# A fused attention and soft mixture kernel: first pair of batches in halves, sums moved from POOL to PE, routing and merge rewritten

## The chip, the cores and the metric

The kernel runs on one core of a Trainium2 chip. The core has TensorE (PE, with its weight loads shown apart as PEld), VectorE (DVE), ScalarE (ACT), GpSimd (POOL) and SyncE (SP), which issues the transfers. The metric is the device time in microseconds from start to end of one execution; the time of a kernel is the median of its runs.

## The reference

```python
def _attn_ref(q, k, v, phi):            # 8 batches, 8 heads, 576 rows, 64 wide; phi has 32 columns
    a = phi - np.max(phi, axis=2, keepdims=True)      # softmax of phi over the 576 rows
    a = np.exp(a)
    a = a / (np.sum(a, axis=2, keepdims=True) + 1e-09)
    k_m = np.einsum('bhsm,bhsd->bhmd', a, k)          # 32 pooled keys and values for each head
    v_m = np.einsum('bhsm,bhsd->bhmd', a, v)
    scores = (1.0 / np.sqrt(q.shape[-1])) * np.matmul(q, k_m.transpose(0, 1, 3, 2))
    ...                                               # softmax over the 32
    return np.matmul(attn, v_m)

def _moe_ref(x, phi, w1, w2):           # x: 4608 x 512; phi: 512 x 32 slots; 8 experts of 4 slots
    logits = x @ phi
    d = exp(logits - logits.max(0)); d /= d.sum(0) + 1e-09     # over the 4608 rows
    slot_input = d.T @ x
    ...                                               # each expert: relu(slot_input[e] @ w1[e]) @ w2[e]
    c = exp(logits - logits.max(1)); c /= c.sum(1) + 1e-09     # over the 32 slots
    return c @ slot_out                               # 4608 x 512
```

The attention output x is never formed. The slot logits come from the attention weights times (v_m times slot phi), and the slot input from the attention weights times the routing weights.

## The kernel before

Work is handed to a small planner, class Plan: every `add(engine, cost, fn, r, w, also, pri, dma)` is one group of instructions with a cost in us, the tiles it reads and writes, and a due time set by `plan.at`. At the end `plan.issue()` goes through the groups by its own costs and so fixes the order of the instructions on each engine and of the transfers in the one DMA queue of SP. Buffers are rings of Slots; a group waits for a slot until its last user is done. The order is set when the program is made. What the chip does later follows that order with semaphores.

The eight batches go in four pairs (bp 0 to 3; g is 0 or 1 in a pair). A batch's rows lie on 128 partitions in four column blocks c (two heads, a = 0 and 1, each), nine rows j per partition. For each batch:

- `pool_phi`: load phi; DVE takes the maximum over j (L511), a PE transpose (L519), a small DVE maximum (L524) and PE matmuls (L533) spread it; ScalarE copies it (L544); POOL subtracts it (L549); ScalarE takes the exponential in place (L555); POOL adds the nine j by a tree of four additions (L562); a PE matmul with a mask of the half partitions (L572) and two DVE operations (L579, L580) give the reciprocal sums.
- `pool_kv`: load k and v; 144 PE matmuls of 64 x 32 weights (L599) accumulate the pooled keys and values in kvbank, of which there is one; ScalarE scales them out (L615, L622); PE transposes (L635, L640); ScalarE copies (L654, L645); PE multiplies the pooled values with the slot phi (L662); ScalarE places the result (L675).
- `load_q`, `q_blocks`: load q, two DVE transposes (L700), one for each half of the columns.

For each c of a pair: `scores` (PE L716, DVE transpose out of PSUM L730), `softmax` (DVE maximum L746, POOL subtract L751, ScalarE exponential L756, DVE sum L761, ScalarE L766, DVE reciprocal L770, POOL multiply L774, DVE transpose L777) and `logits` (PE L785), which accumulates the slot logits of the pair in one PSUM bank. DVE turns those into L (L955). `route` then takes the maximum over the rows for each slot: a strided DVE reduction of L (L803), PE transpose (L810), DVE (L815), PE (L821), DVE subtracts (L829), ScalarE exponential (L837); then 36 matmuls with the attention weights (L849), copies (L861, L865), matmuls (L875, L881), a masked DVE product (L890) and the matmuls that give the pair's unnormalised slot input sip (L909).

After the last pair the four pairs' parts are merged with factors from their maxima (DVE L969 to L1000; L975 is ScalarE's exponential): SIU and SD hold the parts of slot input and denominator, SIM is the merged slot input. The experts follow: `expert_in` (L1064), `hidden`, `expert_out` (L1113) read 32 weight tiles of 1 MB each; `slots` makes the combine weights; the tail multiplies them with the experts' output (L1220) and writes 12 pieces.

Memory: one arena of 44288 columns holds the attention tiles (`stack`) from the bottom up, and the weight tiles (`ws`, 2048 columns each, 19 of them) over the same columns from the top down. A weight load waits until every attention tile under its slot is done.

The first loads have an order of their own:

```python
FIRST = ["phi0", "phi1", "mphi", "q0", "k0", "v0", "q1", "k1", "v1"]
```

`fill` puts matmuls on ones into PE's idle time early (to 25 us of the planner's clock) and before the experts (L476).

Of the kernel before, what the change touches and what calls it, by code (L numbers as in the profile page):

```python
# [252 lines left out]
def kernel(  # L253
# [103 lines left out]
    def stack(shape, n, fifo=False):  # L357
# [37 lines left out]
    kvs = stack([KV_SZ], 2, fifo=True)  # L395
# [14 lines left out]
    C_EXP = 0.8  # L410
# [22 lines left out]
    add(DVE, 1.8, f, r=[ident_b], w=[maskhp_b, maskc_b, rep_b, ones_b])  # L433
# [6 lines left out]
    dmhs = sb("dmh", [NS, 1], 2)  # L440
# [22 lines left out]
    FIRST = ["phi0", "phi1", "mphi", "q0", "k0", "v0", "q1", "k1", "v1"]  # L463
# [37 lines left out]
    def pool_phi(b):  # L501
        pt = phis.tile()
        ph = lambda: pt.ap.rearrange("p (c j m) -> p c j m", c=C, j=J)
        load(
            lambda: pt.ap.rearrange("p (c x) -> p c x", c=C), rows(phi, b), H * S * M * 4, pt,
            pri=first(f"phi{b}"),
        )
        mx, mh, mb, es, rs = pmxs.tile(), pmhs.tile(), pmbs.tile(), pess.tile(), prss.tile()
        add(
            DVE, 2.2,  # L510
            lambda: nc.vector.tensor_reduce(  # L511
                mx.ap, ph().rearrange("p c j m -> p c m j"), axis=AX.X, op=ALU.max
            ),
            r=[pt], w=[mx],
        )
        t0 = b_m.tile()
        add(
            PE, TP,
            lambda: nc.tensor.transpose(t0.ap[:, :P], mx.ap.rearrange("p c m -> p (c m)"), ident),  # L519
            r=[mx, ident_b], w=[t0], also=[mh],  # L520
        )
        add(
            DVE, dve(P),
            lambda: nc.vector.tensor_reduce(  # L524
                mh.ap, t0.ap[:, :P].rearrange("x (a p) -> x a p", a=2), axis=AX.X, op=ALU.max
            ),
            r=[t0], w=[mh],
        )
        t1 = b_m.tile()

        def f():
            for a in range(2):
                nc.tensor.matmul(  # L533
                    t1.ap[HALF * a: HALF * a + HALF, :P],
                    mh.ap[:, a: a + 1].to_broadcast([P, HALF]),
                    ident,
                    start=True,
                    stop=True,
                )

        add(PE, pe(4, HALF, P, tiles=2), f, r=[mh, ident_b], w=[t1], also=[mb])
        add(
            ACT, act(128),
            lambda: nc.scalar.copy(mb.ap.rearrange("p c m -> p (c m)"), t1.ap[:, :P]),  # L544
            r=[t1], w=[mb],
        )
        add(
            POOL, pool_tt(PHI_SZ),
            lambda: nc.gpsimd.tensor_tensor(  # L549
                ph(), ph(), mb.ap.unsqueeze(2).to_broadcast([P, C, J, M]), op=ALU.subtract  # L550
            ),
            r=[mb, pt], w=[pt],
        )
        add(
            ACT, act(PHI_SZ, False), lambda: nc.scalar.activation(pt.ap, pt.ap, AF.Exp),  # L555
            r=[pt], w=[pt],
        )
        tr = trees.tile()

        def f():  # L560
            t = tr.ap
            plus = lambda o, x, y: nc.gpsimd.tensor_tensor(o, x, y, op=ALU.add)  # L562
            plus(t, ph()[:, :, 0:4, :], ph()[:, :, 4:8, :])
            plus(t[:, :, 0:2], t[:, :, 0:2], t[:, :, 2:4])
            plus(t[:, :, 0], t[:, :, 0], t[:, :, 1])
            plus(es.ap, t[:, :, 0], ph()[:, :, 8, :])

        add(POOL, pool_tt(512) + pool_tt(256) + 2 * pool_tt(128), f, r=[pt], w=[es, tr])
        sp = b_m.tile()
        add(  # L570
            PE, pe(2, 128, 2),
            lambda: nc.tensor.matmul(  # L572
                sp.ap[:, :2], es.ap.rearrange("p c m -> p (c m)"), maskhp, start=True, stop=True
            ),
            r=[es, maskhp_b], w=[sp], also=[rs], slack=S_SLACK,
        )

        def f():
            nc.vector.tensor_scalar(rs.ap, sp.ap[:, :2], EPS, None, op0=ALU.add)  # L579
            nc.vector.reciprocal(rs.ap, rs.ap)  # L580

        add(DVE, 0.32, f, r=[sp], w=[rs])
        return pt, ph, rs

    def pool_kv(b, pt, ph, rs, vpb):

        kb = kvs.tile().split(2)
        kv = lambda: kb.ap.rearrange("p (i c x) -> p i c x", i=2, c=C)
# [91 lines left out]
        for r in range(R):  # L680
            add(ACT, act(H * NS), lambda f=f, r=r: f(r), r=[vpp], w=[vpb.part(R * g + r)])
# [594 lines left out]
```

## Time and profile before

| what | value |
|---|---|
| time, median of 3 runs | 222.75 us (222.53 to 223.4) |
| profiled execution | 221.83 us, of which 220.1 us are the span |
| busy: PE, PEld | 172.5, 105.3 us |
| busy: DVE | 135.5 us |
| busy: ACT | 71.4 us |
| busy: POOL | 86.7 us |
| read from HBM, written | 66.65 MB, 9.44 MB |

Busy time is the time in which an engine has an instruction at work, and a wait inside the order of its queue counts as idle. The span runs from the first to the last instruction. In a row of the timeline stand the start, the time it took in us, engine, line, operation, tiles and shapes, and how long the engine was idle before it and for what. In the table of groups stand the busy us of the whole group, the mean ns of one, and the idle time before them.

### The profile page before, as it was taken

Reading aid. Unit: us, or ns where it says so; the run is one execution under the profiler, and the core shown is the slowest. Engines: PE = TensorE matmul, PEld = TensorE weight load, DVE = VectorE, ACT = ScalarE, POOL = GpSimd, SP = SyncE. Lnnn points to the kernel's source line nnn. Section 1 sums busy time; section 2 is a strip of 40 time slices with the busy share of each in tenths; the row PEclk is TensorE's granted clock in tenths of the full one; section 3 lists DMA queues with packets and bytes.
Section 4 is the critical chain, followed back from the end, with each engine's and each line's share of the span. In section 5 each row is a group of like instructions: output and inputs, shape, how many; then the busy total and the mean of one; then the engine's idle time right before and its main releaser. Section 6 shows DMA issues by size and latency. Waiting matters only on the chain.

```text
span 220.1 us, 5624 instructions
## 1 busy us (share of the span) xinstructions
PE 172.5 (78%) x2418; PEld 105.3 (48%) x2418; DVE 135.5 (62%) x230; ACT 71.4 (32%) x182; POOL 86.7 (39%) x85
## 2 busy tenths in 40 slices
PE   8997977695798988598988799629999975599400
PEld 6676745354564654356654387415554340065100
DVE  6825048969459999879658965499102860268500
ACT  2041234542516626337342340201002331168400
POOL 6298019596934992999623641030000000000000
PEclk9999999979699999999969999976999999769755
DMA  6999999999999999999596493999999998049997
GB/s 215 383 395 390 380 392 381 390 380 390 385 388 389 388 406 380 389 392 406 194 410 212 188 420 102 401 350 327 395 413 410 408 409 320 3 179 411 415 415 295
DMA packets 27881, 76.45 MB, mean 347 GB/s; under 512 B 1744, under 2 KB 5840, under 8 KB 27856
## 3 DMA queue, kind: packets, MB, share of 16 engines
q1 hardware_dynamic: 27856, 76.09, 91.1%
q8 instruction: 19, 0.31, 0.6%
q14 instruction: 6, 0.05, 0.1%
HBM read 66.65 MB, written 9.44 MB: 346 GB/s over the span
## 4 chain that ended last, share of the span: by engine, by line
PE 41%; DMA 22%; DVE 14%; POOL 9%; issue 5%; ACT 2%; SPq 1%; DVEq 0%; POOLq 0%
DMA top<-in_q_dram 10%; DMA arena<-in_moe_w_dram 9%; PE bank L1064 7%; PE kvbank L476 6%; PE bank L785 5%; PE scbank L716 4%; PE bank L1220 4%; PE kvbank L599 3%; DMA out_dram<-arena 3%; DVE arena L700 3%; POOL arena L774 3%; POOL arena L562 3%; PE bank L849 2%; PE kvbank L1113 2%; POOL arena L751 2%
## 5 line engine op out<-in xcount | busy, mean ns | idle before, releaser
L549 POOL TENSOR_TENSOR arena<-arena 128x1152 f32<-128x1152 f32 x8 | 21.0, 2632 | 16.0 <-ACT arena L544 13.3
L476 PE MATMUL kvbank<-ones 128*128 128x256 f32 x92 | 25.4, 419 | 2.2 <-ACT arena L622 1.1
L700 DVE STREAM_TRANSPOSE arena<-top 128x1152 f32<-128x1152 f32 x16 | 21.7, 1361 | 7.1 <-DMA top<-in_q_dram 7.1
L774 POOL TENSOR_TENSOR arena<-arena,ssm 128x576 f32<-128x576 f32 x16 | 18.5, 1162 | 15.6 <-DVE ssm L770 15.5
L562 POOL TENSOR_TENSOR arena<-arena 128x128 f32<-128x128 f32 (+2 forms) x32 | 23.4, 731 | 2.3 <-ACT arena L555 0.3
L716 PE MATMUL scbank<-arena 64*64 64x288 f32 x256 | 21.6, 433 | 3.0 <-DVE arena L730 2.5
L785 PE MATMUL bank<-arena 128*128 128x288 f32 x64 | 21.4, 464 | 2.6 <-DVE arena L777 2.6
L751 POOL TENSOR_TENSOR arena<-arena,smx 128x576 f32<-128x576 f32 x16 | 18.4, 1158 | 11.5 <-DVE smx L746 11.5
L599 PE MATMUL kvbank<-arena 64*32 64x128 f32 x1152 | 20.2, 273 | 2.2 <-issue 1.5
L476 PEld LDWEIGHTS kvbank<-ones 128*128 128x128 f32 x92 | 18.1, 207 | 6.7 <-issue 1.6
L511 DVE TENSOR_REDUCE arena<-arena 128x128 f32<-128x1152 f32 x8 | 17.0, 2138 | 5.6 <-DMA arena<-in_phi_dram 5.6
L599 PEld LDWEIGHTS kvbank<-arena 64*32 64x32 f32 x1152 | 16.2, 106 | 6.3 <-issue 3.9
L1064 PE MATMUL bank<-arena,SIM 128*32 128x256 f32 x256 | 16.4, 421 | 3.4 <-DVE SIM L1000 3.4
L1113 PE MATMUL kvbank<-arena 128*32 128x512 f32 x128 | 15.6, 598 | 2.9 <-DMA arena<-in_moe_w_dram 2.9
L730 DVE STREAM_TRANSPOSE arena<-scbank 128x576 f32<-128x576 f32 x16 | 12.2, 765 | 8.9 <-PE scbank L716 8.9
L785 PEld LDWEIGHTS bank<-arena 128*128 128x128 f32 x64 | 12.1, 206 | 8.1 <-DVE arena L777 3.8
L1220 PE MATMUL bank<-sr,cT 128*128 128x512 f32 x36 | 13.2, 505 | 3.1 <-DVE sr L1207 1.4
L1231 DVE COPY arena<-bank 128x512 f32<-128x512 f32 x18 | 11.8, 691 | 4.7 <-DMA out_dram<-arena 2.4
L777 DVE STREAM_TRANSPOSE arena<-arena 128x576 f32<-128x576 f32 x16 | 12.1, 758 | 3.8 <-POOL arena L774 3.7
L716 PEld LDWEIGHTS scbank<-arena 64*64 64x64 f32 x256 | 9.0, 137 | 10.8 <-DVE arena L730 4.5
L756 ACT ACTIVATE arena<-arena 128x576 f32<-128x576 f32 x16 | 11.0, 688 | 8.4 <-POOL arena L751 8.4
L1064 PEld LDWEIGHTS bank<-arena,SIM 128*32 128x32 f32 x256 | 8.6, 121 | 10.7 <-DVE SIM L1000 3.6
(104 smaller groups left out, 234.4 us busy)
## 6 DMA issues: line engine op xcount, KB each, us to landing
arena<-in_moe_w_dram SPq DMA_DIRECT2D x32, 1024.0 KB, 9.9
top<-in_q_dram SPq DMA_DIRECT2D x8, 1152.0 KB, 13.8
arena<-in_k_dram SPq DMA_DIRECT2D x8, 1152.0 KB, 11.2
arena<-in_v_dram SPq DMA_DIRECT2D x8, 1152.0 KB, 13.6
out_dram<-arena SPq DMA_DIRECT2D x12, 768.0 KB, 7.6
arena<-in_phi_dram SPq DMA_DIRECT2D x8, 576.0 KB, 8.7
arena<-in_moe_phi_dram SPq DMA_DIRECT2D x1, 64.0 KB, 4.8
```

The source lines that it names most:

```text
L476: lambda: nc.tensor.matmul(warm.ap, ones, ones.unsqueeze(1).to_broadcast([P, 2, P]), start=True, stop=True,),
L549: lambda: nc.gpsimd.tensor_tensor(ph(), ph(), mb.ap.unsqueeze(2).to_broadcast([P, C, J, M]), op=ALU.subtract),
L562: plus = lambda o, x, y: nc.gpsimd.tensor_tensor(o, x, y, op=ALU.add)
L599: nc.tensor.matmul(acc.ap[M * c: M * c + M, a, : 2 * D], ph()[h0: h0 + HALF, c, j, :], kv()[h0: h0 + HALF, :, c, j * D: j * D + D], start= ...
L700: nc.vector.transpose(qT.ap.rearrange("p (i u y) -> p u i y", i=2, y=Y), qt.ap[:, h * QT_SZ: h * QT_SZ + QT_SZ].rearrange("p (u i x) -> p ...
L716: nc.tensor.matmul(scb.ap[HALF * g: HALF * g + HALF, a, :JY], kb[g].ap[h0: h0 + HALF, i, c].rearrange("p r m -> p (r m)"), qT[g][c // 2].a ...
L751: lambda: nc.gpsimd.tensor_tensor(exv(), exv(), bc(mx), op=ALU.subtract),
L774: lambda: nc.gpsimd.tensor_tensor(exv(), exv(), bc(sm), op=ALU.mult),
L785: nc.tensor.matmul(lp.ap[:, :JY], vpb.ap[:, h, :], aT.ap[:, a * JY: (a + 1) * JY], start=(h == 0), stop=(h == H - 1),)
L1064: nc.tensor.matmul(hb.ap[NS * j: NS * j + NS, :256], SIM.ap[:, 2 * i + c, NS * e: NS * e + NS], wv[:, c, 256 * j: 256 * j + 256], start=(e ...
L1113: nc.tensor.matmul(pacc.ap[NS * x: NS * x + NS, 0, :DM], hT()[:, 4 * t + 2 * i + j, NS * e: NS * e + NS], wv[:, j, t, :], start=(e == 0 an ...
L1220: lambda po=po, i=i, ct=cT[bp, j0]: nc.tensor.matmul(po.ap[:, :DM], ct.ap()[:, i * P: i * P + P], sr.ap, start=True, stop=True),
```

## The change

1. The first pair is worked in two units: column blocks 0 and 1, then 2 and 3. Loads, maxima, subtraction, exponential, sums, pooling and transposes are issued for each unit; the other pairs keep one unit. The functions become methods of a class Batch (`load_phi`, `load_kv`, `load_q`, `turn_q`, `shifted`, `summed`, `pooled`, `turned`). The scores of c wait for the keys of their unit only, and the logits for the values of theirs. In the first loads q stands behind k and v of the unit.
2. The exponentials go to a tile of their own (pes), ordered by j first. The sums over the rows are made by PE: nine matmuls, with a 32-column mask as weights and the exponentials moving, then a ScalarE copy and one small matmul. POOL's tree goes.
3. kvs has three buffers for two; pes is new; the tree's buffer goes.
4. The routing maximum is taken from the logits in PSUM with the slots on partitions; its negative is spread by a matmul with rep, ScalarE's exponential reads PSUM with it as a bias, and DVE transposes the result. MB holds negatives of maxima.
5. In the merge the sums over the first three pairs are made ahead of the last pair's; the last pair's part is added to them with two DVE operations. The copy of one half of the last pair's wt goes from ScalarE to DVE. The zeroing of hTb goes from POOL to DVE.
6. Logits get a due time half a pair later.

```diff
-    dm1s = stack([NS], 2)
+    dTs = stack([JN], 1)
...
-    trees = stack([C, 4, M], 1)
-    pmxs, pmbs, pess = stack([C, M], 2), stack([C, M], 2), stack([C, M], 2)
+    pes = stack([J, C, M], 2)
+    pess = stack([C * M], 1)
+    pmxs, pmbs = stack([C, M], 2), stack([C, M], 2)
...
-    kvs = stack([KV_SZ], 2, fifo=True)
+    kvs = stack([KV_SZ], 3, fifo=True)
...
+        nc.vector.memset(maskw, 0.0)
...
-    FIRST = ["phi0", "phi1", "mphi", "q0", "k0", "v0", "q1", "k1", "v1"]
+    FIRST = [
+        "phi0.0", "phi1.0", "k0.0", "v0.0", "k1.0", "v1.0", "mphi", "q0.0", "q1.0",
+        "phi0.1", "phi1.1", "k0.1", "v0.1", "k1.1", "v1.1", "q0.1", "q1.1",
+    ]
...
+            add(
+                ACT, act(PHI_SZ // self.units, False),
+                lambda: nc.scalar.activation(
+                    pe_.ap[:, :, c0:c1].rearrange("p j c m -> p c j m"), ph(), AF.Exp
+                ),
+                r=[pt.part(u)], w=[pe_.part(u)],
+            )
+        def summed(self, u):
+            pe_, rs, n, o = self.pe, self.rs, self.n, u * self.n
+            s4, sp, es = b_m.tile(), b_m.tile(), pess.tile()
+            def f():
+                for j in range(J):
+                    x = Y * (j % 4)
+                    nc.tensor.matmul(
+                        s4.ap[x: x + Y, :n], maskw,
+                        pe_.ap[:, j, c0:c1].rearrange("p c m -> p (c m)"),
+                        start=(j < 4), stop=(j >= J - 4), tile_position=(0, x),
+                    )
+            add(PE, 0.45, f, r=[pe_.part(u), maskw_b], w=[s4], also=[es])
+            add(ACT, act(n), lambda: nc.scalar.copy(es.ap[:, :n], s4.ap[:, :n]), r=[s4], w=[es])
+            add(PE, 0.2, lambda: nc.tensor.matmul(
+                    sp.ap[o: o + n, :2], es.ap[:, :n], rep[:, 0, :2], start=True, stop=True),
+                r=[es, rep_b], w=[sp], also=[rs])
...
+        r=[*(x.qT[c // 2] for x in pair), *(x.kd.part(x.part(c)) for x in pair)],
...
+        add(PE, 0.96, f, r=[aT, *(vpb.part(4 * u + x) for x in range(4))], w=[lp])
...
+    def route(bp, ex, pair, lp):
+        def f():
+            nc.vector.tensor_reduce(dmx.ap[:, 0:1], lp.ap[:, :JY], axis=AX.X, op=ALU.max)
+            nc.vector.tensor_scalar(dmx.ap[:, 1:5], neg_b.ap, dmx.ap[:, 0:1], None, op0=ALU.mult)
...
+            PE, 0.12, lambda: nc.tensor.matmul(
+                t0.ap[:, :C], rep.rearrange("p a n -> p (a n)"), dmx.ap[:, 1:5], ...
+            DVE, 0.15,
+            lambda: nc.vector.tensor_reduce(dmx.ap[:, 5:6], t0.ap[:, :C], axis=AX.X, op=ALU.min),
+            ACT, act(JN),
+            lambda: nc.scalar.activation(dT.ap, lp.ap[:, :JY], AF.Exp, bias=dmx.ap[:, 5:6]),
+        add(DVE, dve(JN), lambda: nc.vector.transpose(df.ap, dT.ap), r=[dT], w=[df])
...
+            if bp == NSEG - 1 and g == 1:
+                add(DVE, dve(HM) + dve(1), lambda g=g: f_dve(g), r=[wp[g]], w=[wt.part(g)])
...
+        units = 2 if bp == 0 else 1
+        pair = [Batch(2 * bp + g, units) for g in range(2)]
+        for u in range(units):
+            for x in pair:
+                plan.at(bp - 1.15 + 0.5 * x.g + 0.25 * u, 8)
+                x.load_phi(u); x.shifted(u); x.load_kv(u); x.summed(u); x.pooled(u); x.turned(u, vpb)
+            plan.at(bp - 0.45 + 0.3 * u)
+            for x in pair:
+                x.load_q(u)
...
+            plan.at(bp + 0.25 * c + 0.5, 15)
+            logits(c, aT, vpb, pair[0].part(c), lp)
...
+        nc.vector.tensor_mul(rst.ap[:, 0], wtp.ap[:, 4 * NS: 5 * NS], cf.ap[:, nl])
+        nc.vector.tensor_add(rst.ap[:, 0], rst.ap[:, 0], st.ap)
+        nc.vector.reciprocal(rst.ap[:, 0], rst.ap[:, 0])
+        nc.vector.tensor_mul(rst.ap[:, 1], rst.ap[:, 0], cf.ap[:, nl])
+        nc.vector.tensor_mul(sip_c.ap, sip_c.ap, bc(rst.ap[:, 0]))
...
+        nc.vector.tensor_mul(SIT.ap, part, bc(rst.ap[:, 1]))
+        nc.vector.tensor_add(
+            SIM.ap.rearrange("p c (e x) -> p c e x", e=E)[:, :, :, :SE],
+            SIT.ap.rearrange("p c (e s) -> p c e s", e=E),
+            sip_c.ap.rearrange("p c (e s) -> p c e s", e=E),
...
-    add(POOL, 2.0, lambda: nc.gpsimd.memset(hTb.ap, 0.0), r=[SIM], w=[hTb])
+    add(DVE, 2.4, lambda: nc.vector.memset(hTb.ap, 0.0), r=[SIM], w=[hTb])
```

More of the change, by code (lines that the diff above doesn't have):

```diff
@@ L403 @@
     mphd_b = keep("mphd", [P, C, 2, NS])
-    ident, maskhp, maskc, rep, ones, mphd = (
-        x.ap for x in (ident_b, maskhp_b, maskc_b, rep_b, ones_b, mphd_b)
+    ident, maskw, maskc, rep, ones, mphd = (
+        x.ap for x in (ident_b, maskw_b, maskc_b, rep_b, ones_b, mphd_b)
     )
@@ L409 @@
     WC = 0.45
-    C_EXP = 0.8
     S_SLACK = 0.6
@@ L422, in f @@
         nc.vector.tensor_reduce(
-            maskhp, ident.rearrange("p (c x) -> p c x", c=2), axis=AX.X, op=ALU.add
+            maskw[:, :2], ident.rearrange("p (c x) -> p c x", c=2), axis=AX.X, op=ALU.add
         )
@@ L439 @@
     prss = sb("prs", [P, 2], 3)
-    dmhs = sb("dmh", [NS, 1], 2)
+    dmxs = sb("dmx", [P, 6], 2)
+    neg_b = keep("neg", [P, C])
+    add(
+        DVE, 0.1,
+        lambda: nc.vector.tensor_scalar(neg_b.ap, maskc, -1.0, None, op0=ALU.mult),
+        r=[maskc_b], w=[neg_b],
+    )
     L = [keep(f"L{i}", [P, JN]) for i in range(NBP)]
@@ L498, in rows @@
         return x[b].rearrange("h (p j) y -> (h p) (j y)", j=J).rearrange("(c r) x -> r c x", r=P)
[L501 to L538, printed above, removed]
-                )
[L541 to L583, printed above, removed]
@@ L709, in scores @@
+    def scores(c, pair, ex):
         scb = b_s2.tile()
@@ L879, in f @@
                     )
-            for g in range(2):
-                nc.tensor.matmul(
-                    wtp.ap[:, 4 * NS: 5 * NS],
-                    wt.ap[:, g, HM: HM + 1].to_broadcast([P, P]), rep[:, 0, :],
-                    start=(g == 0), stop=(g == 1),
-                )
         add(PE, 1.3, f, r=[wt, rep_b], w=[wtp], also=[wtb])
@@ L898, in route @@
         )
-        add(
-            ACT, act(32),
-            lambda: nc.scalar.copy(SD.ap[:, bp, :], wtp.ap[:, 4 * NS: 5 * NS]),
-            r=[wtp], w=[SD.part(bp)],
-        )
+        if bp < NSEG - 1:
+            add(
+                ACT, act(32),
+                lambda: nc.scalar.copy(SD.ap[:, bp, :], wtp.ap[:, 4 * NS: 5 * NS]),
+                r=[wtp], w=[SD.part(bp)],
+            )
         sip = b_m.tile()
@@ L915, in f @@
                     )
-        add(PE, 0.6, f, r=[wtb, *vm], w=[sip])
+        add(PE, 0.6, f, r=[wtb, *(x.vm for x in pair)], w=[sip])
         if bp == NSEG - 1:
-            return sip
+            return wt, wtp, sip
         add(
@@ L950 @@
             plan.at(bp + 0.25 * c, 15)
-            scores(c, qT, kb, ex)
+            scores(c, pair, ex)
             aT = softmax(c, ex)
-            logits(c, aT, vpb, lp)
-        add(
-            DVE, dve(JN), lambda lp=lp, bp=bp: nc.vector.transpose(L[bp].ap, lp.ap[:, :JY]),
-            r=[lp], w=[L[bp]],
-        )
+            plan.at(bp + 0.25 * c + 0.5, 15)
+            logits(c, aT, vpb, pair[0].part(c), lp)
         plan.at(bp + (1.2 if bp < NBP - 1 else 1.0), 10)
-        sip = route(bp, ex, vm)
+        last = route(bp, ex, pair, lp)
     plan.at(20)
@@ L965 @@
     st = keep("st", [P, NS])
+    rst = keep("rst", [P, 2, NS])
     nl = NSEG - 1
+    wt, wtp, sip = last
     def f():
-        nc.vector.tensor_reduce(m4.ap, MB.ap.rearrange("p b n -> p n b"), axis=AX.X, op=ALU.max)
+        nc.vector.tensor_reduce(m4.ap, MB.ap.rearrange("p b n -> p n b"), axis=AX.X, op=ALU.min)
         nc.vector.tensor_tensor(
```

447 lines of the change are left out of this document (276 added, 171 removed).

## Prediction

> **What bounds the kernel now.** I read the page's head first, then the chain of waits, then a table of stages that I cut at four instants, and last the timeline at the cuts. The head:
>
> ```profile
> span 220.1 us, 5624 instructions
> ...
> DMA  6999999999999999999596493999999998049997
> GB/s 215 383 395 390 380 392 381 390 380 390 385 388 389 388 406 380 389 392 406 194 410 212 188 420 102 401 350 327 395 413 410 408 409 320 3 179 411 415 415 295
> ...
> arena<-in_moe_w_dram SPq DMA_DIRECT2D x32, 1024.0 KB, 9.9
> top<-in_q_dram SPq DMA_DIRECT2D x8, 1152.0 KB, 13.8
> ...
> arena<-in_phi_dram SPq DMA_DIRECT2D x8, 576.0 KB, 8.7
> ```
>
> The transfers run at 380 to 415 GB/s nearly everywhere. They fail in two places: slices 20 to 25 (104.5 to 137.6 us), and slices 34 to 36, between the last weight and the first output. The cuts:
>
> ```profile
> 26.23 1.53 PEld L599 LDWEIGHTS kvbank<-arena 64*32 64x32 f32 x110 [0.48 <-DMA arena<-in_v_dram]
> 31.31 1.46 PE L716 MATMUL scbank<-arena 64*64 64x288 f32 x16
> 64.41 1.20 PE L716 MATMUL scbank<-arena 64*64 64x288 f32 x16
> 135.83 0.48 DVE L955 STREAM_TRANSPOSE L<-bank 128x288 f32<-128x288 f32 x1 [1.90 <-PE bank L785]
> 147.32 0.29 DVE L1000 TENSOR_TENSOR SIM<-arena,st 128x128 f32<-128x128 f32 x1
> 187.44 1.11 PE kvbank L1113 x8
> ```
>
> 31.3 is the first scores matmul of pair 0 (the two first batches), 64.4 that of pair 1, 135.8 the end of the last logits (I call it E), 147.6 the merged slot input SIM, 187.4 the last expert matmuls. Busy time between the cuts (engine, busy us, instructions; then clock, DMA share, GB/s):
>
> ```profile
> core 0: us, PE busy (x) PEld busy (x) DVE busy (x) ACT busy (x) POOL busy (x), PEclk, DMA share, GB/s
> 4.30:31.30 27.00, 23.98 (x387) 18.31 (x385) 12.83 (x14) 6.88 (x17) 11.63 (x13) 1.00 1.06 386
> 31.30:64.40 33.10, 25.37 (x564) 16.95 (x562) 23.67 (x35) 14.05 (x34) 25.59 (x23) 0.90 1.06 386
> 64.40:114.60 50.20, 43.06 (x770) 27.27 (x769) 43.53 (x69) 22.55 (x67) 34.58 (x31) 0.97 0.98 372
> 114.60:135.80 21.20, 19.43 (x170) 12.71 (x170) 15.00 (x26) 6.52 (x20) 9.16 (x8) 1.00 0.66 255
> ```
>
> VectorE (DVE) holds the attention stage: from 4.3 to 135.8 it works 95.0 us (the first four rows) of 131.5, only 12.8 of the first 27.0, and 87% of 64.4 to 114.6. After E the DMA rules, but it is late because weight slots come free only as attention lets go of its memory:
>
> ```profile
> 56.07 3.22 SPq L458 DMA_DIRECT2D arena<-in_moe_w_dram  x1
> ...
> 126.20 0.37 SPq L458 DMA_DIRECT2D arena<-in_moe_w_dram  x1
> 135.83 0.88 SPq L458 DMA_DIRECT2D arena<-in_moe_w_dram  x2
> ```
>
> Between the first two of these rows 14 of the 32 weight loads are issued; the 15th and 16th go out at E itself. The 18 that are left by then are 18.9 MB, 46 us at 410 GB/s (2.56 each), and 187.4 - 135.8 is 51.6. So the end follows E, until the DMA has no idle time left to give.
>
> **The change, part by part.**
>
> **Halves of the first pair.** Before, v of batch 1, the last of 8.26 MB (two batches, each of 576 KB of phi and 1152 KB each of q, k and v), is waited for until 26.2, and scores start 5.1 us behind. Afterwards scores of c = 0, 1 need only the first halves, 4.13 MB: 26.2 - 4.13/0.386 = 15.5, plus 3 us of q transposes and waits (an estimate between 0 and the 5.1 us from v): 18.5, 12.8 us earlier. The second halves land at 26.2 as before. The halves add the instructions of 2 more units (a second transpose, reduction, reciprocal each, the big ones at half size), which I put at 2 us of DVE; where units go through the single kvbank one behind another, ScalarE's copies stand between them, but that is work in a stretch in which DVE waits anyway. The first pair's DMAs become 16 for 8, in a queue whose issue is hidden behind the landing; q moves behind k and v, and the slot weights (mphi) behind them too, so POOL's copies of mphi (mphd) come later, beside POOL's first subtractions, and only the vpp matmuls wait for them.
>
> How much of 12.8 reaches E? DVE has 95.0 + 2 = 97 us to do. Up to 18.5 it does 6.7, at the first row's rate (12.83 in 27.0). The other 90.3 take 114 us at the share of 31.3 to 135.8 (82.2 of 104.5, 0.79), which gives E at 133; 104 at the 0.87 of the third row, E at 122. Which of them depends on the next part.
>
> **Phi sums by PE.** POOL's tree goes, PE and ScalarE take it up:
>
> ```profile
> DMA top<-in_q_dram 10%; DMA arena<-in_moe_w_dram 9%; PE bank L1064 7%; PE kvbank L476 6%; PE bank L785 5%; PE scbank L716 4%; PE bank L1220 4%; PE kvbank L599 3%; DMA out_dram<-arena 3%; DVE arena L700 3%; POOL arena L774 3%; POOL arena L562 3%; PE bank L849 2%; PE kvbank L1113 2%; POOL arena L751 2%
> L562 POOL TENSOR_TENSOR arena<-arena 128x128 f32<-128x128 f32 (+2 forms) x32 | 23.4, 731 | 2.3 <-ACT arena L555 0.3
> L572 PE MATMUL bank<-maskhp,arena 128*128 128x2 f32 x16 | 2.6, 235 | 0.0
> L849 PE MATMUL bank<-arena 64*32 64x288 f32 x144 | 7.5, 408 | 1.2 <-DVE m L969 1.2
> L519 PE MATMUL bank<-ident,arena 128*128 128x128 f32 x8 | 2.6, 321 | 6.2 <-DVE arena L511 5.9 <-DVE prs L579 0.3
> ```
>
> 23.4 us leave POOL, which alternates with DVE in every softmax (subtract, multiply); 3% of the span, 6.6 us, are on the chain of waits itself. In its place stand 9 matmuls of 128 x 32 weights with 128 columns, a copy and a 2-column matmul per batch. Low end: as L849, 7.5/144 = 0.05 us each, 0.5; high end: as L519 one behind another, 9 x 0.32 = 2.9. I take 0.6, since column-tiled L849 is the nearer form. With 0.24 for the small matmul and less the 0.33 of L572 it is 0.5 a batch net, 4 us on PE, 22 at the high end; PE has 16.6 us idle from 31.3 to 135.8. The change adds a wait there, the small matmul's for ScalarE's copy, with the kv matmuls and next scores queued behind it on PE, and DVE waiting for those; before, the same matmul waited for the tree's last addition. So I take DVE's share in between, at 0.83: 90.3/0.83 = 108.8, E at 18.5 + 108.8 = 127.3. E comes some 9 us earlier, at 127; bounds 3 and 14 us.
>
> [...]
>
> ```profile
> 105.89 1.17 PE bank L785 x4
> 107.06 0.87 PE kvbank L599 x48
> ```
>
> These two neighbours in the chain of waits differ in tiling (128*128, then 64*32), and no time shows between them. [...]
>
> **Exponentials past the mask, third kv buffer.** ScalarE's exp writes another tile (pes) in another order at the same size: nothing. That and a third kv buffer cost memory. By the diff's sizes the attention tiles grow from 34436 to 40932 of 44288 columns; with slots of 2048 columns, 4 weight slots are free from the start now and 1 afterwards. Once the last kv is used 10 are free now and 9 then, after the last scores 13 and 13. The DMA idles (410 - 255)/410 of the fourth row, 8 us, so I take 0 for the loss, and 3 x 2.56 = 7.7 us if nothing else makes it up.
>
> **Routing and merge,** E to SIM, 11.8 us now:
>
> ```profile
> 139.17 1.65 PE L849 MATMUL bank<-arena 64*32 64x288 f32 x36 [1.16 <-DVE m L969]
> 142.86 0.69 DVE L890 TENSOR_TENSOR arena<-bank,maskc 128x512 f32<-128x512 f32 x1 [1.84 <-PE bank L881]
> 144.38 2.02 POOL L1046 MEMSET arena<- 128x2304 f32 x1 [11.25 <-PE bank L909]
> 144.53 1.90 DVE L990 TENSOR_SCALAR st<-st 128x32 f32<-128x32 f32 x1
> 149.47 0.17 DVE L1148 TENSOR_SCALAR csm<-csm 128x9 f32<-128x9 f32 x1
> L579 DVE TENSOR_SCALAR prs<-bank 128x2 f32<-128x2 f32 x8 | 1.1, 141 | 2.0 <-PE bank L572 2.0
> 147.63 0.04 issue
> L837 ACT ACTIVATE arena<-arena 128x288 f32<-128x288 f32 x4 | 1.8, 455 | 0.7 <-DVE arena L829 0.7
> ```
>
> To the start of L849: 3.34 now. Then: reduction 0.48 (as L955, which reads the same PSUM columns), negative 0.14 (L579), matmul 0.24 (L572), small minimum 0.14, exp 0.46 (L837), transpose 0.48, six hand-overs at 0.04 (the issue row): 2.18. Gain 1.2. Further from their forms, these could be 0.5 more or less together. L849, copies (half of them moved to DVE) and L890 keep their time. From L890's end (143.55) to SIM's (147.6) it is 4.1 now: L990 sits 1.90 beside POOL's memset and ends with it, where its like, L1148, takes 0.17. Then: five small operations on DVE, some 1.2 (between 0.14 and 0.29 each), beside the sip matmuls, and two like L1000, 0.29 each, with hand-overs 1.9. Gain 2.2; E to SIM 8.4. The memset goes to DVE, behind SIM: 2 us, taken as on POOL, in front of DVE's routing work, behind which only the experts' hidden layer could wait, after the 16 us of its input matmuls. The slots freed at SIM come 3.4 us nearer to E; of the 5.5 us by which 51.6 exceeds the 46 of pure transfer I take 1.7 as saved (0 to 3.4).
>
> **Sum.** Last experts at 127 + 51.6 - 1.7 = 176.9 instead of 187.4; the tail of 32.7 us is untouched. Span 209.6, 10.5 less. The profiled execution took 221.83, the median of the runs is 222.75, 0.92 above: 222.75 - 10.5 = 212.2.
>
> **The rivals.**
> (1) The start is eaten. On the chain stands
>
> ```profile
> 22.68 14.10 DMA top<-in_q_dram
> ```
>
> q of batch 2, landing at 36.8, and its place behind 12.4 MB is not moved by halving. If pair 1 stays where it is, E comes only 3 us earlier: 218.0 with the merge. Against it: pair 1's scores start only at 64.4, long behind that landing, after pair 0's logits have had DVE and POOL.
> (2) The DMA floor. 33.1 MB at 386 GB/s from 4.3 to 90, then 32 loads at 2.56 us: 172, 173.4 with the landing; 206.1 of span, 208.7. It needs E at 123 or before, which is DVE at 0.87.
> (3) Slower: prefetch starves. If E stays and the three lost slots are missing at E, 11 loads are in instead of 14, and the last lands 7.7 later: 222.75 + 7.7 - 1.7 = 228.7. It decides once E moves by less than 6 us with all three missing. Against it: 10 against 9 slots, and the 8 idle us. PE at its high end (22 us against 16.6 idle) would help it along.
> (4) Nothing moves but the merge, and that is drowned: 221 to 223.
>
> **How the numbers follow.** Forecast 212.2 (E 5 to 12 us earlier, 209.5 to 216.5): 0.54. Rival 1 (216.5 to 221): 0.17. Rival 2 (208 to 209.5): 0.12. Rival 3: 0.11. Rival 4: 0.06. The range 208.0 to 219.5 leaves out rivals 3 and 4 and the upper edge of rival 1. A change of 0.5%, 1.1 us, is about what three runs from 222.53 to 223.4 can tell. Faster 0.83, same 0.06, slower 0.11.
>
> **What would show it.** First scores at 17 to 20 us; last logits at 123 to 131; SIM 8 to 9 us behind, the small scalar operation in the merge under 0.3; the 9 sum matmuls in 0.4 to 0.9; GB/s under 300 in no more than two slices before the last weight; last experts at 174 to 181. The prediction is wrong if first scores come early and the last logits do not, or if the slices between 100 us and E stay empty and only 11 or fewer weight loads are out at E.

## The result, and the profile after

The changed kernel takes 236.51 us (median of 4 runs, 234.51 to 239.87); the kernel before, beside it, 222.64 (222.41 to 223.4). The ratio is 1.0587, interval 1.0477 to 1.0697: slower, where 212.2 was forecast. The profiled execution shown here took 239.87, the longest of the four; its marks are read against its own span, 238.1 us. It is a disturbed run, and so are the profiled ones of one unit, POOL's tree, routing alone, the nine, the one long and the tiny unused matmuls, and the six-matmul sums with one unit: marks read from these profiles are late by some microseconds against the undisturbed runs that give the ratios.

From the page: the head, the slices, the shares of the chain of waits, and the costliest group.

```profile
span 238.1 us, 6024 instructions
...
PE 191.1 (80%) x2604; PEld 116.8 (49%) x2604; DVE 138.6 (58%) x250; ACT 77.0 (32%) x209; POOL 62.2 (26%) x54
...
PEclk9999999798789999598598899997999999659855
DMA  6999769989986998199623899999999999009997
GB/s 199 369 383 387 264 233 381 386 304 392 380 316 204 329 370 297 28 405 406 271 57 125 338 414 406 408 394 352 418 409 406 409 409 396 17 40 413 414 414 305
...
q8 instruction: 20, 0.33, 0.6%
...
PE 66%; DMA 11%; DVE 6%; issue 6%; ACT 5%; POOL 1%; SPq 0%; DVEq 0%; ACTq 0%; POOLq 0%
...
L670 PE MATMUL kvbank<-arena 64*32 64x128 f32 x1152 | 28.3, 289 | 8.5 <-issue 7.9
```

And the pooling matmuls in the kernel before:

```profile
L599 PE MATMUL kvbank<-arena 64*32 64x128 f32 x1152 | 20.2, 273 | 2.2 <-issue 1.5
```

The chain was PE 41%, DMA 22%, DVE 14%, POOL 9%; now PE holds 66% of it. POOL's 24 us less bring no gain here. The pooling matmuls, 1152 as before (L599 then, L670 now), take 28.3 us for 20.2, and 7.9 us in front of them PE had nothing to execute ("issue"). Ahead of the last weights the DMA moves under 300 GB/s in nine slices (1, 5, 6, 13, 16, 17 and 20 to 22), where it was five before (1, 20, 22, 23 and 25).

The stages, cut at the same events (first scores, pair 1's scores, 21.4 us before the last logits, E, the end of the last logits), and the whole stretch, with the busy us of PE, PEld, DVE, ACT and POOL, then clock, DMA share and GB/s; below it the whole stretch of the kernel before:

```profile
4.30:27.80 23.50, 20.28 (x246) 14.44 (x246) 7.92 (x13) 5.87 (x21) 4.06 (x6) 1.00 1.03 369
27.80:69.10 41.30, 35.48 (x658) 24.01 (x656) 27.44 (x41) 16.78 (x50) 16.70 (x12) 0.88 0.94 337
69.10:133.00 63.90, 53.61 (x999) 35.39 (x998) 46.06 (x74) 26.66 (x77) 28.83 (x20) 0.87 0.68 245
133.00:154.40 21.40, 20.78 (x177) 14.02 (x177) 15.75 (x28) 6.75 (x20) 9.16 (x9) 1.00 1.02 412
4.30:154.40 150.10, 130.15 (x2074) 87.85 (x2075) 97.16 (x154) 56.05 (x166) 58.75 (x45) 0.91 0.86 314
```

```profile
4.30:135.80 131.50, 111.84 (x1887) 75.25 (x1886) 95.03 (x143) 50.01 (x136) 80.96 (x75) 0.96 0.97 360
```

The stretch is 18.6 us longer and PE works 18.3 us longer in it, at a clock of 0.91 for 0.96; DVE works 2.1 us more. At full clock PE's times would be some 118 and 107 us (an estimate, time by clock), so about 11 of the 18.3 us are added work and about 7 are the slower clock. All of the loss of this execution, 18.0 us of span, is made before E. What PE waited for up to E, after and before (line waited for: us in total, times, longest):

```profile
PE kvbank L670 <- issue: 7.9, 4, 3.2
...
PE bank L714 <- issue: 2.0, 1, 2.0
```

```profile
PE kvbank L599 <- issue: 1.5, 2, 0.8
```

With 0.6 at L637 the waits for instructions are 10.5 us after and 1.5 before; PE's other waits together shrink. So 131.5 = 111.8 + 1.5 + 18.2 has become 150.1 = 130.2 + 10.5 + 9.4. The timeline shows what such a wait looks like; the other rows are marks that the prediction named:

```profile
9.52 4.04 PE L486 MATMUL kvbank<-ones 128*128 128x256 f32 x10
13.50 0.52 PE L637 MATMUL bank<-arena,maskw 128*32 128x64 f32 x18
13.95 2.17 PE L670 MATMUL kvbank<-arena 64*32 64x128 f32 x72
...
27.84 1.20 PE L779 MATMUL scbank<-arena 64*64 64x288 f32 x16
...
89.45 0.84 PE L637 MATMUL bank<-arena,maskw 128*32 128x128 f32 x18
90.22 0.94 PE L670 MATMUL kvbank<-arena 64*32 64x128 f32 x48
91.09 0.38 PE L647 MATMUL bank<-rep,arena 128*128 128x2 f32 x2
91.40 1.27 PE L670 MATMUL kvbank<-arena 64*32 64x128 f32 x66
95.91 1.10 PE L670 MATMUL kvbank<-arena 64*32 64x128 f32 x30 [3.23 <-issue]
...
99.66 2.13 PE L779 MATMUL scbank<-arena 64*64 64x288 f32 x16
...
154.42 0.46 DVE L868 TENSOR_REDUCE dmx<-bank 128x1 f32<-128x288 f32 x1 [1.99 <-PE bank L852]
...
162.83 0.29 DVE L1088 TENSOR_TENSOR SIM<-arena 128x128 f32<-128x128 f32 x1
```

The nine sum matmuls (18 in the trace, each with a weight load) run in 0.84 us and the pooling follows at once; 114 matmuls into the pooling run, in the middle of a group, PE stands 3.23 us with nothing to execute. The scores behind take 2.13 us for the usual 1.20: from 94.8 to 101.6 us the granted clock is 0.50. On the chain that ended last:

```profile
62.03 1.85 issue
...
92.68 3.23 issue
...
109.66 2.01 issue
...
112.37 2.13 PE scbank L779 x16
...
126.94 2.29 issue
...
130.29 2.18 PE bank L852 x4
...
185.43 18.80 DMA arena<-in_moe_w_dram
204.28 1.98 PE kvbank L1201 x8
```

Four such waits are links of the chain itself, and groups behind them run at about half their rate (the 16 scores matmuls take 2.13 us for 1.20; four of L852 take 2.18, and 1.17 elsewhere on the chain). Behind E the rest follows as it did: last experts at 204.28, 49.9 us after E (51.6 before), and 33.8 us to the end (32.7).

### The profile page after: what moved, and what is told of

The parts are those of the page before. It is cut to its first block, busy times and chain, and to the rows that moved or that the text cites. A ratio compares the mean times of both kernels' runs of the same rounds, so it can differ in the third digit from the quotient of the medians.

```text
span 238.1 us, 6024 instructions
## 1 busy us (share of the span) xinstructions
PE 191.1 (80%) x2604; PEld 116.8 (49%) x2604; DVE 138.6 (58%) x250; ACT 77.0 (32%) x209; POOL 62.2 (26%) x54
## 4 chain that ended last, share of the span: by engine, by line
PE 66%; DMA 11%; DVE 6%; issue 6%; ACT 5%; POOL 1%; SPq 0%; DVEq 0%; ACTq 0%; POOLq 0%
PE kvbank L670 10%; PE bank L852 9%; PE scbank L779 9%; PE kvbank L486 8%; DMA arena<-in_moe_w_dram 8%; PE bank L1152 7%; PE bank L1308 3%; DMA out_dram<-arena 3%; PE bank L915 3%; PE bank L637 2%; PE kvbank L1201 2%; PE bank L747 2%; PE bank L714 2%; PE bank L596 2%; PE bank L957 2%
## 5 line engine op out<-in xcount | busy, mean ns | idle before, releaser
L670 PE MATMUL kvbank<-arena 64*32 64x128 f32 x1152 | 28.3, 289 | 8.5 <-issue 7.9
L614 POOL TENSOR_TENSOR arena<-arena 128x1152 f32<-128x1152 f32 (+1 forms) x10 | 21.5, 2148 | 43.6 <-ACT arena L607 43.6
L670 PEld LDWEIGHTS kvbank<-arena 64*32 64x32 f32 x1152 | 21.3, 111 | 11.7 <-issue 10.3
L841 POOL TENSOR_TENSOR arena<-arena,ssm 128x576 f32<-128x576 f32 x16 | 18.5, 1159 | 31.3 <-DVE ssm L837 31.3
L486 PE MATMUL kvbank<-ones 128*128 128x256 f32 x70 | 23.5, 470 | 3.3 <-ACT arena L694 2.2
L779 PE MATMUL scbank<-arena 64*64 64x288 f32 x256 | 23.2, 452 | 0.8 <-DVE dmx L883 0.6
L852 PE MATMUL bank<-arena 128*128 128x288 f32 x64 | 22.7, 494 | 0.0
L818 POOL TENSOR_TENSOR arena<-arena,smx 128x576 f32<-128x576 f32 x16 | 18.5, 1159 | 12.0 <-DVE smx L813 12.0
L1201 PE MATMUL kvbank<-arena 128*32 128x512 f32 x128 | 16.6, 628 | 3.5 <-DMA arena<-in_moe_w_dram 3.5
L486 PEld LDWEIGHTS kvbank<-ones 128*128 128x128 f32 x70 | 14.8, 230 | 7.6 <-ACT arena L694 3.0
L572 DVE TENSOR_REDUCE arena<-arena 128x128 f32<-128x1152 f32 (+1 forms) x10 | 17.2, 1728 | 0.0
L852 PEld LDWEIGHTS bank<-arena 128*128 128x128 f32 x64 | 13.5, 228 | 5.5 <-issue 1.9
L687 ACT ACTIVATE arena<-kvbank,prs 128x128 f32<-128x128 f32 (+1 forms) x20 | 6.2, 360 | 22.5 <-PE kvbank L670 14.0
L828 DVE TENSOR_REDUCE ssm<-arena 128x18 f32<-128x576 f32 x16 | 11.7, 740 | 1.7 <-ACT arena L823 1.7
```

What stands on the lines that cost most here:

```text
L486: lambda: nc.tensor.matmul(warm.ap, ones, ones.unsqueeze(1).to_broadcast([P, 2, P]), start=True, stop=True,),
L572: lambda: nc.vector.tensor_reduce(mx.ap[:, c0:c1], ph().rearrange("p c j m -> p c m j"), axis=AX.X, op=ALU.max),
L614: lambda: nc.gpsimd.tensor_tensor(ph(), ph(), mb.ap[:, c0:c1].unsqueeze(2).to_broadcast([P, c1 - c0, J, M]), op=ALU.subtract,),
L670: nc.tensor.matmul(acc.ap[M * c: M * c + M, a, : 2 * D], pe_.ap[h0: h0 + HALF, j, c, :], kv()[h0: h0 + HALF, :, c, j * D: j * D + D], star ...
L779: nc.tensor.matmul(scb.ap[HALF * g: HALF * g + HALF, a, :JY], pair[g].kd.ap[h0: h0 + HALF, i, c].rearrange("p r m -> p (r m)"), pair[g].qT ...
L818: lambda: nc.gpsimd.tensor_tensor(exv(), exv(), bc(mx), op=ALU.subtract),
```

## The experiments

Each is compared with runs of the kernel before on the same chip; brackets are intervals. E, waits for instructions up to E ("issue") and PE's busy time from 4.3 us to E come from each one's profile.

### The parts undone one by one

**One unit for all pairs:** the changed kernel with `units = 1`.

> The changed kernel with the first pair in one unit, as the others (q still behind k and v in the first loads). Theory PE (TensorE's own work, its stalls for instructions and its half clock set the end of the last logits, E): the halves cost about 4.4 us of doubled 72-matmul groups and some 2 us of second transposes, so about 228 us (225 to 231), E at 146 to 149. Theory feed (the halves release batch 0's phi buffer late, batch 2's phi is issued at 30.5 us instead of 18.4, and the loads starve from 24 to 36 us): nearly all comes back, 219 to 223 us, E at 136 or before, no slice under 350 GB/s between 5 and 60 us.

1.0135 [1.0032, 1.0238]; E 145.7, issue 7.4, PE 120.4. The halves cost 4.5 points, and with them go 9.8 us of PE's time; 7.4 us of issue stay.

**POOL's tree back, halves kept:**

```diff
-                for j in range(J): ... nc.tensor.matmul(s4.ap[x: x + Y, :n], maskw, ...)
+                plus(t, ph[:, :, 0:4, :], ph[:, :, 4:8, :])   # and three more additions on POOL
```

> The changed kernel with the phi sums by POOL's tree again, on the new tile of exponentials, halves kept. Theory PE: 8 to 10 us of PE work and part of the 10 us of stalls go: 222 to 228 us, the stalls of PE marked issue in the kv matmuls fall from 7.9 to under 4 us. Theory feed: the start is as in the changed kernel, 233 to 238 us, and POOL's 23 us are hidden.

1.0371 [1.0247, 1.0496]; E 149.1, issue 6.7, PE 122.3. The PE sums cost some 2 points beside the halves, and the halves cost by themselves.

**Neither halves nor PE sums:** both edits together; exponentials in pes, three kvs buffers, routing and merge stay.

> The changed kernel with one unit and POOL's tree: what is left are the third kv buffer, the separate tile of exponentials, q behind k and v, the later due time of the logits, and routing and merge. Theory PE and theory feed both say 218 to 222 us. If instead the memory (1 free weight slot instead of 4) or the due time of the logits is what costs, it stays over 226 us.

0.9986 [0.9944, 1.0029]; E 134.6, issue 4.9, PE 112.1, last experts at 186.4, 51.8 behind E. The loss is gone, and no gain is left: halves and PE sums together make the loss.

**Routing and merge alone,** put into the kernel before.

> The kernel before with the new routing and merge alone (maxima from PSUM, negatives, merge prepared ahead, zeroing of hTb on DVE). If these are worth what the trace of the changed kernel shows (E to SIM 8.8 us instead of 11.8): 219.5 to 221.5 us, E unchanged at 134 to 137. If the end is set by transfers that do not depend on SIM: 222 to 223 us.

1.005 [0.9993, 1.0107]. E came at 140.5, later than the 134 to 137 expected, with 4.1 us of issue. SIM's last operation starts 8.4 us behind E (140.5; 148.9), as in the changed kernel, for 11.5 before; the last experts at 192.2 stand 51.7 behind E, as before. The shorter merge is real, and no gain from it shows.

**A longer merge:** in the kernel before, one product of the merge is written 12 times.

```diff
-        nc.vector.tensor_mul(SIT.ap, last, bc(cf.ap[:, nl]))
+        for _ in range(12):
+            nc.vector.tensor_mul(SIT.ap, last, bc(cf.ap[:, nl]))
```

> The kernel before with SIM made about 3 us later (one product of the merge written 12 times instead of once). If the time between E and SIM is hidden behind the weight loads: a ratio of 1.000 to 1.004 and last experts 51 to 53 us behind E. If SIM is on the path: 1.012 to 1.016, and then the shortened merge of the changed kernel is worth as much the other way.

1.0185 [1.0132, 1.0239], 4.1 us, for 3.84 us by which SIM moved: last experts 40.4 us after SIM, 39.8 before. So a longer merge moves the experts' end in full, while the shorter one alone did not move it. In the kernels with the shorter merge the last experts stand 49.7 to 56.3 us behind E, so that distance is no fixed bound; what sets it beside SIM is open.

### Order and buffers

**The planner's costs as measured** (pooling of halves at twice its cost, sums 0.8 and 0.5, small matmul 0.3).

> The changed kernel with the planner told what the trace showed: a half unit's kv matmuls cost as much as a whole unit's (72 matmuls in 2.17 us, 144 in 2.24), the nine sum matmuls 0.8 us (0.5 for a half), the small matmul 0.3. Only the order changes. Theory order (the planner's order is made for a PE faster than the real one): 222 to 230 us. Theory PE work: the work is the same, 232 to 238 us.

1.059 [1.048, 1.07], as the change. The planner's wrong costs are not the cause. Its profile repeats the marks of the changed kernel: E 154.6, issue 10.1, PE 127.6, clock 0.91.

**Four phi buffers for two,** in the changed kernel.

> The changed kernel with four phi buffers instead of two (and so no weight slot free from the start). Theory feed (phi loads of the next batches wait behind the late exponentials of the second halves, and all loads behind them in the one queue): batches 2 and 3 get their phi before 25 us, no slice under 350 GB/s between 5 and 45 us, 222 to 230 us. Theory PE: the loads come earlier and nothing follows, 232 to 238 us.

1.0332 [1.0228, 1.0436]; E 147.0, issue 6.4. Here 2.5 points come back. SP's queue issued the phi of batch 2 at 30.45 in the changed kernel, at 18.41 before, since it waits there 13.3 us for a buffer.

**The same with POOL's tree** (halves kept).

> The changed kernel with POOL's tree and four phi buffers: of the three costs found so far (sums on PE 0.022 to 0.027 of the time before, doubled kv work 0.013, starved loads 0.025) only the doubled kv work is left. If they add up: a ratio of 1.005 to 1.02. If halves cost in another way (order, second transposes): 1.02 to 1.04. If the early start is worth something once these are gone: under 1.00.

1.0746 [1.0676, 1.0817]; E 150.0, issue 10.4. With the tree, more phi buffers made it worse than either alone, and it has as many waits for instructions as the changed kernel with no sum matmul on PE. That late phi loads starve the stage is not supported, and how such buffers act through the order stays open.

### One cost at a time, in the kernel before

**Pooling of batches 0 and 1 in two runs of half the heads.**

```diff
-        for js in (range(0, 3), range(3, 6), range(6, 9)):
+        for x in range(n):        # n = 2 for the first two batches, cs its half of the heads
+            for js in (range(0, 3), range(3, 6), range(6, 9)):
```

> The kernel before with the kv matmuls of batches 0 and 1 issued as two runs of 72 (column blocks 0 and 1, then 2 and 3) instead of one of 144; the same matmuls, the same costs told to the planner. If the array takes as long for 72 of four tile positions as for 144 of eight, PE gets 4.4 us of work more and nothing else changes. Theory PE: 225 to 228 us. If that stretch has PE time to spare: 222 to 223.5 us. If the run of 72 takes half the time, no change and 1.1 us each.

1.0134 [1.0033, 1.0234]; E 140.2, issue 0.9. The pooling of a batch in it, and in the kernel before:

```profile
15.83 3.75 PE L599 MATMUL kvbank<-arena 64*32 64x128 f32 x144
```

```profile
15.78 2.24 PE L599 MATMUL kvbank<-arena 64*32 64x128 f32 x144
```

The same 144 matmuls take 3.75 for 2.24 us; a half uses only four of the eight tile positions. In the changed kernel 72 take 2.17. For two batches that is 3.0 of the 4.4 us of E. The rest is not in these matmuls; the clock up to E was 0.94 for 0.96. Of the 4.5 points that the halves cost with the sums on PE, this split explains 1.3; where the others arise was not isolated.

**Nine unused sum matmuls a batch,** in front of the pooling; POOL's tree stays.

```diff
+            for j in range(J):
+                x = Y * (j % 4)
+                nc.tensor.matmul(
+                    s4.ap[x: x + Y, :P], rep[:, 0, :], ph()[:, :, j, :],
+                    start=(j < 4), stop=(j >= J - 4), tile_position=(0, x),
+                )
```

> The kernel before with the nine sum matmuls of each batch added, their result unused, POOL's tree kept: PE gets about 0.8 us of work and 36 instructions more for each batch, and nobody waits for them. Theory PE (work and instruction stalls): 226 to 231 us. If it is the new wait (matmuls, copy, matmul, one behind another) that costs: 222 to 224 us.

1.0266 [1.0158, 1.0374]; E 145.4, 9.6 us later than in the kernel before, with DVE's work the same (95.3 us for 95.0). Only PE got more to do; one more PSUM buffer is taken, as in the next two runs.

**One unused matmul of 512 columns a batch** at that place; the order on every engine is otherwise that of the run above.

> The kernel before with one matmul of 512 columns for each batch in place of the nine sum matmuls of the run before, its result unused: about as much PE time (0.8 to 0.9 us a batch by the 512-column rows of the tail) with 4 instructions instead of 36. If PE's time is what costs: as the nine sums, a ratio of 1.02 to 1.03 to the kernel before. If it is the number of instructions and the stalls for them: 1.00 to 1.01.

225.08 us against 225.07 of the kernel before (medians, without an interval; the fastest runs 220.76 and 222.44); E 138.1.

**Nine unused matmuls a batch that move only 2 columns;** the same order again.

> The kernel before with the nine unused matmuls of each batch again, but moving 2 columns instead of 128: the same number of PE instructions and weight loads in the same order, hardly any PE array time. Theory supply (PE runs out of instructions when many short ones follow one another, and the idle time halves its clock): ratio 1.015 to 1.03 to the kernel before, issue stalls of PE over 4 us. Theory PE time: 1.000 to 1.008.

231.14 us against 223.7 (medians, without an interval; the fastest runs 226.47 and 222.97); E 146. The waits for instructions up to E and the added matmuls' groups of the three, in that order:

```profile
PE kvbank L610 <- issue: 3.6, 1, 3.6
PE bank L563 <- issue: 3.6, 1, 3.6
...
L563 PE MATMUL bank<-arena,rep 128*32 128x128 f32 x144 | 7.5, 291 | 5.1 <-issue 3.6 <-ACT arena L555 1.5
```

```profile
PE scbank L722 <- issue: 0.8, 1, 0.8
PE kvbank L605 <- issue: 0.6, 1, 0.6
...
L561 PE MATMUL bank<-arena,ones 128*128 128x512 f32 x16 | 8.7, 625 | 0.6 <-ACT arena L555 0.6
```

```profile
PE kvbank L610 <- issue: 4.1, 1, 4.1
PE bank L563 <- issue: 3.9, 1, 3.9
...
L563 PE MATMUL bank<-arena,rep 128*32 128x2 f32 x144 | 3.3, 183 | 4.6 <-issue 3.9 <-ACT arena L555 0.6
```

This tells the theories apart, as far as medians and fastest runs can. 8.7 us of PE time in 16 long matmuls cost nothing that either shows. 3.3 us in 144 tiny ones cost 7 us by the medians and 3.5 by the fastest runs, where 7.5 us in 144 of 128 columns cost 6 and 5.3. So it is in the main the number of instructions, not their work, and it shows as two waits of 4 us in which PE has nothing to execute. The granted clock goes the same way: over the fastest runs it was 0.94 with the long ones and 0.90 with the short and the tiny. (The long one also differs in tiling, 128*128; but the waits lie inside groups, and no time shows where the tiling changes: with the tiny ones, L563 of 128*32 ends at 43.99 by its row and L610 of 64*32 starts at 43.92.)

### The changed kernel with fewer sum instructions

**Each unit's nine replaced by one matmul of 512 columns,** same order on every engine; the sums leave out most rows.

```diff
-                for j in range(J): ... nine matmuls of n columns
+                nj = 512 // n
+                nc.tensor.matmul(s4..., ones, pe_.ap[:, :nj, c0:c1]..., start=True, stop=True)
```

> The changed kernel with one matmul of 512 columns in place of each unit's nine sum matmuls, in the same order on every engine; its sums leave out most of the rows. About 1.1 us of PE time for 0.8, 4 instructions for 36. Theory supply: ratio 1.02 to 1.04 to the kernel before (the changed kernel 1.059), issue stalls of PE under 8 us. Theory PE time: 1.055 to 1.07.

1.01 [1.0052, 1.0147]; E 139, issue 3.0, clock 0.99. Its sums take more time on PE (11.0 us) than the nine (7.7), and 4.9 of the 5.9 points are gone, better than expected. Of the 15.4 us by which E comes earlier, 7.5 are waits for instructions and 9.4 are PE's busy time (120.8 for 130.2) at the faster clock; the other waits are 1.5 us longer. What stays, with the halves still in, is near the 1.3 of the split pooling alone.

**Full sums, in three matmuls of 384 columns (192 in a half) and three small ones,** two units.

```diff
-                    nc.tensor.matmul(s4.ap[x: x + Y, :n], maskw, pe_.ap[:, j, c0:c1]..., tile_position=(0, x))
+                for j in range(0, J, 3):
+                    nc.tensor.matmul(s4.ap[:, : 3 * n]..., maskw, pe_.ap[:, j: j + 3, c0:c1]...)
```

> The changed kernel with its two units, where each unit's sums are made in full by three matmuls that move 3 row groups at once (384 columns, 192 for a half) and three small ones: 6 and 6 matmuls and weight loads less... in numbers 6 matmuls for 10, so 8 PE instructions fewer per unit and about 1 us more PE time per full unit. Supply theory (short instructions in front of the kv runs make PE wait): below the changed kernel's 1.059, at 1.01 to 1.03 of the kernel before, with under 6 us of waits for instructions before the last logits. Rival (PE's time is what counts): 1.06 to 1.08.

1.0418 [1.0363, 1.0472]; E 143.2, issue 0.7. The waits went, as expected, but the time missed the 1.01 to 1.03:

```profile
4.30:143.20 138.90, 127.09 (x1983) 87.90 (x1983) 98.36 (x154) 58.11 (x166) 58.68 (x45) 0.99 0.92 333
...
L636 PE MATMUL bank<-arena,maskw 128*128 128x384 f32 (+1 forms) x60 | 19.6, 466 | 4.2 <-ACT arena L623 4.2
L646 PE MATMUL bank<-rep,arena 128*128 128x2 f32 (+1 forms) x60 | 7.0, 233 | 0.0
```

The sums now cost 26.6 us of PE at a clock of 0.99 (11.1 in the changed kernel, at 0.91), and PE works 127.1 of 138.9 us.

**The same with one unit.**

> The same sums in three long and three small matmuls, with one unit for all pairs. With nine short matmuls and one unit it was 1.0135. Supply theory: 0.985 to 1.005, since POOL is relieved and PE does not wait. Rival (PE's time): 1.015 to 1.03.

1.0598 [1.0527, 1.067]: a clear miss. Sums 27.4 us, E 150.5, and 4.2 us of issue on top:

```profile
4.30:150.50 146.20, 129.29 (x1957) 86.41 (x1955) 97.06 (x146) 53.96 (x144) 58.36 (x43) 0.94 0.86 316
```

So PE's plain work counts too once there is enough of it: the stretch is PE's 129.3, the 4.2, and 12.7 of all other waits. Nine short matmuls with one unit had 120.4, 7.4 and 13.6. With these sums two units are the better by 1.8 points, where with nine short ones they were the worse by 4.5: the parts do not add, and what the halves are worth hangs on how PE's queue is filled around them.

**Two kvs buffers for three,** in three places: with one unit and the tree, with that and an unused 512-column matmul a batch, and with the six-matmul sums.

> One unit and POOL's tree as in an earlier run, with two kv buffers instead of three (4 weight slots free from the start instead of 1). If slots that are free early shorten the end: E as there (133 to 137 us), last experts under 50 us behind E, ratio 0.97 to 0.99 to the kernel before. If they are made up for before E anyway: 0.995 to 1.005.

> The fastest version so far (one unit, POOL's tree, two kv buffers, new routing and merge) with one unused matmul of 512 columns for each batch. If long matmuls keep PE's clock up, and that is worth more than their time: ratio 0.975 to 0.99 to the kernel before, time at half clock before E under 15 us (30.7 there). If not: 0.992 to 1.01.

> As the run with one unit and sums in six matmuls, and two kvs buffers for three, which with the tree gave 0.9923. Supply theory: 0.98 to 1.0. If the gain of two buffers was a matter of that one order alone: 1.0 to 1.03, as with the unused 512-column matmul (1.0278).

0.9923 [0.9873, 0.9974], 1.0278 [1.0218, 1.0338] and 1.0735 [1.0679, 1.079]. The first is the only version faster than both kernels, by 0.8%; its interval overlaps that with three buffers. The others miss: the long matmul, free in the kernel before, cost 3.5 points here, with E 145.7 and 6.9 us of issue. Two buffers are no gain in general. Why the waits came back there is open, and so few instructions for the sums do not always keep them away.

## Why the prediction was wrong, step by step

**What holds the attention stage** is the step that failed. The prediction gave the stage to DVE and forecast E from DVE's share, between 0.79 and 0.87, at 127. DVE's work came out as put (97.2 us for 97), its share as 0.65, and E as 154.4. In all kernels run DVE's work up to E is 95 to 99 us, while E lies anywhere from 134.6 to 154.6. PE's queue, in the order that the planner fixed, held it: nine unused matmuls a batch, for which nobody on DVE waits, moved E by 9.6 us in the profile and the time by 2.7%. Over the kernels run, the stretch up to E is PE's busy time, 112 to 130 us, plus its waits for instructions, 1 to 10, plus 9 to 19 us of all other waits. (Such a sum can be written for any engine; it is the unused matmuls that show which one counts.) "PE has 16.6 us idle" was read as room; these other waits did not go under 9.4 in any profile, so of the 18.2 in the kernel before some 9 could be filled, as far as these runs show. The view that would have told is the windows table with PE beside DVE: 111.8 of 131.5 is 85%, DVE's 95.0 is 72%.

**The sums by PE** are the mis-sized term. Forecast: 0.6 us a batch, 4 us net on PE, absorbed. Measured: 0.84 us for a full unit, inside the 0.4 to 0.9 given; over the stage 7.7 + 3.4 - 2.6 = 8.5 us net. What the term left out: with 36 more short instructions beside a run of 288, PE stood at times with nothing to execute, 1.85 to 3.23 us at a time in the changed kernel and 3.6 to 4.1 with the unused short ones. The unused matmuls put that at 2.7% for the kernel before, and the one long matmul in the changed kernel at 4.9 points of its 5.9. That the lack lies in the fetching of PE's instructions is what the trace of the changed kernel points to: the page has 20 transfers of 16 KB in the instruction queue, and the four waits for instructions of 1 us or more up to E, which end at 63.87, 95.91, 111.68 and 129.23, end 1.4 to 1.6 us after one of them (62.28, 94.53, 110.32 and 127.74). No run changed the fetching itself, and the kernel before has 19 such transfers and no such wait over 0.8 us. The nine are not the only cause of such waits: kernels without any sums on PE have them too (6.7 us with halves and POOL's tree, 10.4 with four phi buffers besides), and why they fall where they do is open. Nor is it isolated how the clock hangs on the waits and on the long matmuls: 10.4 us of waits went with a clock of 0.95 up to E there, 10.1 with 0.91 in the changed kernel with corrected costs.

Behind the waits of the changed kernel the clock was lower: the scores behind 3.23 us of wait take 2.13 us for 1.20, and the shorter waits of 2.0 and 2.3 us were followed by the same (the chain's rows at 112.37 and 130.29), with a granted clock of 0.50 from 111.8 to 118.6 and from 128.9 to 132.3. But in the kernel before it was 0.50 too from 111.2 to 114.6 us, where from 92 us on PE was never idle for more than 0.8 us at a time; what sets the clock is not shown.

**The halves** were to bring the first scores to 18.5; they came at 27.84 (31.31). The rows from 9.52 show why: fill matmuls hold PE until 13.5, a half's pooling takes 2.17 us, not half of 2.24, and the units follow each other through the one kvbank with fills and copies between. The 2 us of DVE were right; the PE work of two more units was not counted and is the larger part: 9.8 us of PE busy with the sums on PE, 10.1 with the tree, each with some slower clock in it (0.91 for 0.92, and 0.89 for 0.92, up to E).

**Where the tiling changes,** no time shows: L637 (128*32) ends at 90.29 by its row and L670 (64*32) starts at 90.22. Ends of matmuls are modelled in these rows, so a small time could hide in them.

**Routing and merge** were right in size and wrong in worth. E to SIM, counted to where SIM is ready as the prediction did, is 8.7 us (8.4 forecast), the small operation L1060 at 0.18, as forecast under 0.3. Of the 1.7 us booked as saved nothing shows: with the merge alone changed, the last experts stand 51.7 behind E, 51.6 before.

**The end follows E:** right in kind (49.9 behind it, 49.9 forecast), and the tail within 1.1 us. That the very number came is in part luck, since the merge for which it was booked saved nothing alone.

**The rivals.** The other three kept E at 135.8 or before it. The slower case had 0.11 and the wrong mechanism: it lacked prefetched weights at E, but the DMA ran at 412 GB/s in the last 21 us before E, and 15 weight loads were out ahead of E, for 14 before. Its added clause, PE at its high end of 22 us against 16.6 idle, was nearer; it was priced as work and given no case of its own. The stated sign of error did appear: scores early (by 3.5 us), last logits late. So did nine slices under 300 GB/s before the last weight, where at most two had been named.

## What to carry to other kernels

Before work is given to an idle-looking engine, look at the queue it enters: PE, busy 85% of the stage, had about half of its idle time to give here (9 of 18.2 us), and the rest belonged to waits that stayed. On PE count instructions as well as time, above all short ones in front of long runs of small matmuls (here 3.3 us of tiny ones cost more than 8.7 us of long ones), and in the profile look for "issue" in the middle of a group. Splitting a packed run of tiles into halves need not halve its time; here a half took 1.9 to 2.2 us, the whole 2.24.

## What the runs showed of the hardware

- Nine 2-column matmuls a batch (144 in the trace, 3.3 us in all) cost 7 us of the kernel by the medians and 3.5 by the fastest runs; a 512-column one a batch, 8.7 us in all, cost nothing by either. PE stood up to 4.1 us with nothing to execute.
- The four waits of PE for instructions of at least 1 us up to E in the changed kernel (1.85 to 3.23 us) end 1.4 to 1.6 us after a transfer of 16 KB in the instruction queue.
- 72 matmuls on four of eight tile positions take 2.17 us, 144 on all eight 2.24.
- POOL's load fell from 81 to 59 us in the stage, and the kernel with the tree put back (one unit) is 1.5 points faster than with sums on PE.
